# A step of the first stage emitted a slot later, with more buffers and another spacing of the weight work

## Chip, cores and metric

The kernel runs on 1 core of one Trainium2 chip. The metric is the device time of one execution in microseconds (us). Before the change it is 957.8 us, the median of 3 runs (956.14 to 958.7).

## What is computed

Linear attention with 128 random features, then two feed-forward layers. Cut to what matters here:

```
def phi(x):                                   # features of keys and of queries
    proj = einsum('bhsd,md->bhsm', x, omega)
    h = proj - sum(x*x)/2
    return exp(h - max(h, axis=-1)) / sqrt(m)
kv  = einsum('bhsm,bhsd->bhmd', phi(k), v)    # per batch and head: values by features
num = einsum('bhsm,bhmd->bhsd', phi(q), kv);  den = einsum('bhsm,bhm->bhs', phi(q), sum(phi(k)))
x = num / den                                 # (4, 8, 576, 64) -> 2304 tokens x 512
x = (silu(xn @ w_gate) * (xn @ w_val)) @ w_out        # xn: rms norm of x; d_ff 1536
y = (h * cos(h)) @ w_out2,  h = x @ w_in              # d_ff 2048
```

## The kernel before, in words

Tokens go in 18 tiles of 128. The first stage walks 24 slots: in each one tile begins, 18 tiles of keys (named k0 to k17) and the first 6 tiles of queries (q0 to q5, in the slots 6, 9, 12, 15, 20 and 23). `begin(s)` of a slot emits `project` (L426: 16 matmuls on TensorE into two banks of PSUM, one for each half of the heads) and `features` (L435 and L437: VectorE reduces the maximum of each head out of the bank, two reductions a tile, and ScalarE runs 8 exponentials a tile, for which it needs those maxima). A key tile's features then go into `kv_product` (L591 before the change, 32 matmuls: values by features), which before the change is emitted in the slot after the tile's own. A query tile passes 7 further steps in later slots (`query_step`): 1 transposes its features (L444) and copies them (L454 on VectorE, L452 on ScalarE), 2 multiplies them with the sums of a batch and divides (L466, L476 to L478), 3 squares (L485), 4 takes the root (L489, L490, GpSimd), 5 scales (`norm`, L494, VectorE, at the head of its slot), 6 and 7 turn the result and split it (L504, L516, L518).

Within a slot the order is: loads that are due, step 5, `begin`, the other steps of older tiles, `kv_product`, and last `wts.tick(n)`. The tick takes n steps of the preparation of the first twelve chunks of weights, each 128x512 and loaded as 64-bit numbers, which `front` and `split` turn into a high and a low part. The steps run in a fixed cycle of eight, one cycle a chunk: L190 (VectorE, reads the tile W, writes f); L214 of the chunk before (ScalarE); L193 (VectorE; nothing for two chunks in three); L217 of the chunk before (GpSimd); L195 (VectorE); `exponent` of the next chunk (ScalarE, L182 or L184, writes W); L204 (VectorE); L209 (GpSimd). The tile W has one buffer. So `exponent` is the sixth step of a cycle, and the L190 that reads its W is the first of the next, three steps on. What the ticks have not done by the end of the slots is drawn later, at a rate (`pace`), between the products of layer 1.

Each engine has one queue and works through it in the order in which the code emits. Banks: `project` and the turned tile share four banks in a ring ("wa" and "wb"), so a `project` waits until the bank was read by the exponentials of two slots earlier, and, in the slots after a turned tile, until L518 has read that one. Features have 5 buffers (3 of the pool "att", 2 of "values"), values 3 (`vt`). SyncE's queue issues the loads; a load of values waits for the `kv_product` that read the buffer.

After the slots the first products of layer 1 follow (L833, L872 to L874, L886), with the steps of the other 12 query tiles among them; then the rest of the two layers, where TensorE is busy nearly all the time.

Of the kernel before, what the change touches and what calls it, by code (L numbers as in the profile page):

```python
# [33 lines left out]
F32 = mybir.dt.float32  # L34
# [10 lines left out]
P = 128  # L45
NB = 384
# [10 lines left out]
def attention_then_ffn(ctx: ExitStack, tc: tile.TileContext, qT, kT, v, omT, wc1, rms_g, wc2, out, B, H, S, D):  # L57
    nc = tc.nc
    M = omT.shape[1]
    DM = H * D  # L60
    KD = DM // P
    HP = H // 2
# [21 lines left out]
    def parts(t):  # L84

        pr, i = divmod(t, TPP)
        if i == MIX:
            return [(2 * pr, 0, P // 2), (2 * pr + 1, P // 2, P // 2)]
        return [(2 * pr + (i > MIX), 0, P)]
# [312 lines left out]
    wts = Weights()  # L402
# [144 lines left out]
    with tc.manual_schedule():  # L547
        fp = ctx.enter_context(tc.tile_pool(name="fp", bufs=2, reuse_waits="tile"))
        early = ExitStack()
        ap = early.enter_context(tc.tile_pool(name="att", bufs=2, side="right", reuse_waits="tile"))  # L550
        depth = {"gain": 1, "raw": 3, "feat": 3, "mx": 6, "den": 4}
        with_keys = {"raw": 1, "feat": 2}
        turn_of = {"raw": 0, "feat": 0}
        keys = [True]

        def att_tile(what, shape, dt, name):
            own = depth.get(what, 2)
            if keys[0] and what in with_keys:
                n = turn_of[what] % (own + with_keys[what])
                turn_of[what] += 1  # L560
                if n >= own:
                    return vp.tile(shape, dt, tag=what, name=name, bufs=with_keys[what])
            return ap.tile(shape, dt, tag=what, name=name, bufs=own)

        kv = [ap.tile([P, KVW], F32, name=f"kv{b}", bufs=1) for b in range(B)]
        NV = 3
        values = ExitStack()
        vp = values.enter_context(tc.tile_pool(name="values", bufs=1, side="right", reuse_waits="tile"))
        vt = [vp.tile([P, H, D + 1], F32, name=f"v{i}", bufs=1) for i in range(NV)]
        att = Attention(att_tile, "q", kv)  # L570


        acc = {}

        def load_v(t):
            if t < NTILE:
                nc.sync.dma_start(vt[t % NV][:, :, 0:D], v[t])

        def kv_product(t, i):
# [3 lines left out]
            for r in range(2):  # L583
# [3 lines left out]
                for h in range(HP):  # L587
                    hh = 2 * h + r
                    for c in range(2):
                        half_c = slice(c * M // 2, (c + 1) * M // 2)  # L590
                        nc.tensor.matmul(  # L591
                            acc[b, r][half_c, h * P:h * P + D + 1], att.e["k", t, r][p0:p0 + n, h, half_c],
                            vt[t % NV][p0:p0 + n, hh, :],
                            start=begin and h == 0, stop=end, skip_group_check=True)
# [148 lines left out]
        SLOTS = len(tiles)  # L743
# [3 lines left out]
        begins, then = {}, {}  # L747
        for s, (nm, t) in tiles.items():
            if nm == "k":
                for i in range(len(parts(t))):  # L750
                    then.setdefault(s + 1 + i, []).append((1, kv_product, t, i))
                then.setdefault(s + 2 + i, []).append((0, load_v, t + NV))
            else:
                for i in range(1, 8):
                    at = s + i + (s >= SLOTS - 1 or i > 1)
                    then.setdefault(at, []).append((-i, query_step, t, i))
# [6 lines left out]
        def load_ahead(s):  # L763
            at = order.index(s) if s in tiles else -1
            if at >= 0 and at + AHEAD[0] < len(order) and at + AHEAD[0] not in asked:
                asked.add(at + AHEAD[0])
                att.load(*tiles[order[at + AHEAD[0]]])

        def older(s, *steps):
            for step in steps:  # L770
                for k, f, *args in then.get(s, []):
                    if k == step:
                        f(*args)

        def begin(s):
            if s in tiles:
                att.project(*tiles[s])
                for r in range(2):
                    att.features(*tiles[s], r)
# [21 lines left out]

        for s in range(SLOTS):
            load_ahead(s)
            if s in (0, 1):
                load_v(s + 1)
                wts.load(s + 1, nc.sync)
            if s == 3:
                att.load_gain()
            older(s, 0, -5)
            begin(s)  # L810
            older(s, -7, -6, -4, -3, -1, -2, 1)
            if s:
                wts.tick(5 if s < 6 else 1 if s < 14 else 4 if s + 1 < SLOTS else 0)


        att.tag = "w"
# [48 lines left out]
        def silu(blk, f, ps):  # L865
            a = row(F32, f"gv{blk}_{f}")
            nc.scalar.activation(a, ps, AF.Silu)
            return a
# [82 lines left out]
        for n, (g, blk, f, first, last) in enumerate(steps):  # L951
# [9 lines left out]
            s = SLOTS + 2 * n  # L961
# [3 lines left out]
            a = silu(blk, f, ps)  # L965
# [466 lines left out]
```

## Time and profile before

| | |
|---|---|
| median of 3 runs | 957.8 us (956.14 to 958.7) |
| the profiled execution | 955.29 us, its span 953.5 us, mean granted clock 0.996 |
| TensorE (PE) busy | 929.5 us, 97% of the span |
| VectorE (DVE), ScalarE (ACT), GpSimd (POOL) | 713.4, 537.1, 415.5 us |
| chain that ended last | PE 43% of the span, beginning only at 497 us |

The span begins with the first instruction and ends with the last; 1.8 us of the execution lie around it. A row of a timeline gives start, duration and how many instructions it merges, and in brackets the idle time of the engine before it and what ended that.

### The profile page before, as it was taken

What the parts mean: (1) busy time and instruction counts of PE and PEld (TensorE: products, weight loads), DVE (VectorE), ACT (ScalarE), POOL (GpSimd) and SP (SyncE); (2) the same over time, 40 slices, a digit from 0 to 9 for tenths busy, and PEclk for the clock granted to TensorE, in tenths of its full rate; (3) what the DMA queues carried; (4) which work ended last, traced back from release to release, by engine and by line L of the source; (5) the groups of instructions that cost most, each with busy time, mean ns of one, the idle gap of its engine ahead of it and who ended that gap; (6) DMA issues with size and microseconds to landing.
All of it is one profiled execution on the core that took longest, in us unless ns stands there. A gap on an engine that the chain in (4) does not pass through costs nothing. (4 is left out here: it accounts for less than half of the span.)

```text
span 953.5 us, 17373 instructions
## 1 busy us (share of the span) xinstructions
PE 929.5 (97%) x6337; PEld 866.7 (91%) x6337; DVE 713.4 (75%) x1159; ACT 537.1 (56%) x1155; POOL 415.5 (44%) x377
## 2 busy tenths in 40 slices
PE   8988999999999999999999999999999999999998
PEld 7777998989999999999999998889888988988997
DVE  5797777878854685585876658996799787786766
ACT  7898776756535443435363645664655565464443
POOL 2143387467836975376583763320343220240000
PEclk9999999989999999999999999999999999999999
DMA  9774378777796988766989693967622767307554
GB/s 290 201 192 164 134 264 292 264 257 271 231 346 226 400 288 294 268 200 202 386 297 383 231 374 130 355 211 251 210 93 101 251 205 285 124 21 282 191 227 160
DMA packets 112214, 227.71 MB, mean 239 GB/s; under 512 B 28160, under 2 KB 63616, under 8 KB 112128
## 3 DMA queue, kind: packets, MB, share of 16 engines
q1 hardware_dynamic: 110832, 222.34, 67.5%
q10 hardware_dynamic: 1296, 4.26, 1.4%
q8 instruction: 50, 0.82, 0.4%
q14 instruction: 36, 0.29, 0.1%
HBM read 156.04 MB, written 70.52 MB: 238 GB/s over the span
## 5 line engine op out<-in xcount | busy, mean ns | idle before, releaser
L1253 PE MATMUL o_ps<-w,o 128*128 128x512 f32 x864 | 226.0, 393 | 0.7 <-DVE o L1056 0.7
L209 POOL TENSOR_TENSOR f<-f,raw 128x512 f32<-128x512 f32 x68 | 94.4, 1388 | 229.2 <-DVE raw L204 199.2
L1253 PEld LDWEIGHTS o_ps<-w,o 128*128 128x128 f32 x864 | 159.7, 188 | 24.5 <-DVE o L1056 1.1
L217 POOL TENSOR_TENSOR w<-b,w 128x512 fp32r<-128x512 f32 x88 | 115.5, 1318 | 137.0 <-ACT w L214 113.7
L833 PE MATMUL gv_ps<-xhl,w 128*128 128x384 f32 x576 | 109.3, 338 | 1.3 <-DVE eT L454 1.1
L833 PEld LDWEIGHTS gv_ps<-xhl,w 128*128 128x128 f32 x576 | 101.6, 190 | 2.4 <-DVE eT L454 1.6
L1152 PE MATMUL y<-t,w 128*128 128x384 f32 x576 | 102.0, 334 | 0.3 <-POOL w L217 0.3
L1152 PEld LDWEIGHTS y<-t,w 128*128 128x128 f32 x576 | 100.0, 188 | 0.6 <-POOL w L217 0.6
L1053 ACT CAST o<-turns 128x384 fp32r<-128x384 f32 x96 | 47.4, 513 | 93.4 <-DVE turns L1234 93.4
L1045 PE MATMUL Xh<-T,w 128*128 128x384 f32 x432 | 87.4, 336 | 1.6 <-ACT h L1198 1.6
L1045 PEld LDWEIGHTS Xh<-T,w 128*128 128x128 f32 x432 | 76.8, 188 | 9.7 <-ACT h L1198 4.1
L1045 PE MATMUL X<-T,w 128*128 128x384 f32 x432 | 80.7, 334 | 0.0
L1045 PEld LDWEIGHTS X<-T,w 128*128 128x128 f32 x432 | 75.4, 188 | 0.0
L214 ACT CAST w<-b 128x512 fp32r<-128x512 f32 x88 | 50.5, 580 | 31.9 <-DVE b L274 24.8
L1056 DVE TENSOR_TENSOR o<-turns,o 128x384 fp32r<-128x384 f32 x96 | 60.0, 639 | 8.5 <-ACT o L1053 8.1
L886 PE MATMUL y_ps<-t,w 128*128 128x384 f32 x288 | 61.8, 350 | 0.3 <-ACT t L873 0.3
L1019 ACT ACTIVATE turns<-turns,half_pi 128x768 f32<-128x768 f32 (+1 forms) x50 | 45.7, 914 | 22.8 <-DVE turns L1223 22.7
L1045 PE MATMUL Yh<-B,w 128*128 128x384 f32 x288 | 58.0, 336 | 0.0
L1223 DVE SCALAR_TENSOR_TENSOR turns<-turns,r 128x768 f32<-128x768 int32 (+1 forms) x50 | 56.4, 1128 | 1.7
L1234 DVE TENSOR_TENSOR turns<-h,turns 128x768 f32<-128x768 f32 (+1 forms) x50 | 55.1, 1101 | 2.5 <-ACT turns L1019 2.5
L190 DVE TENSOR_SCALAR f<-W 128x512 int32<-128x512 int32 x68 | 44.0, 647 | 15.1 <-ACT W L182 6.5
L1045 PEld LDWEIGHTS Yh<-B,w 128*128 128x128 f32 x288 | 51.4, 188 | 4.2 <-ACT h L1198 0.4
(116 smaller groups left out, 1804.6 us busy)
## 6 DMA issues: line engine op xcount, KB each, us to landing
T<-T_dram SPq DMA_DIRECT2D x48, 768.0 KB, 7.1
raw<-wc SPq DMA_DIRECT2D x60, 512.0 KB, 5.1
B<-yh_dram SPq DMA_DIRECT2D x21, 768.0 KB, 5.5
kept<-f SPq DMA_DIRECT2D x56, 256.0 KB, 5.1
b<-kept SPq DMA_DIRECT2D x56, 256.0 KB, 4.8
B<-x_dram SPq DMA_DIRECT2D x15, 768.0 KB, 6.7
x_dram<-xhl SPq DMA_DIRECT2D x12, 768.0 KB, 5.7
s<-x_dram SPq DMA_DIRECT2D x24, 384.0 KB, 5.6
```

Source lines behind the costliest of these rows:

```text
L209: nc.gpsimd.tensor_tensor(f32(f), f32(f), rest, op=ALU.add)
L214: nc.scalar.copy(t[:, 0, to], src)
L217: nc.gpsimd.tensor_tensor(t[:, 1, to], src, f32(t[:, 0, to]), op=ALU.subtract)
L833: nc.tensor.matmul(o, w[i], x[j], start=n == 0, stop=n == len(terms) - 1)
L886: nc.tensor.matmul(yacc[blk][e], w[:, i, e * P:(e + 1) * P], t[:, j], start=first and i + j == 0, stop=last and j == 1)
L1045: nc.tensor.matmul(o, w[:, i, c + kk * P:c + (kk + 1) * P], x[:, j, kk], start=begin and n == 0, stop=n == 5, skip_group_check=True)
L1053: nc.scalar.copy(t[:, 0], a)
L1056: engine.tensor_tensor(t[:, 1], a, f32(t[:, 0]), op=ALU.subtract)
L1152: nc.tensor.matmul(acc[e], w[:, i, e * P:(e + 1) * P], t[:, j], start=f == fs[0] and i + j == 0, stop=f == fs[-1] and j == 1)
L1223: nc.vector.scalar_tensor_tensor(r, a, -TWO_PI_LO, b, op0=ALU.mult, op1=ALU.add)
L1234: at(mu, lambda: nc.vector.tensor_tensor(r, h, r, op=ALU.mult))
L1253: nc.tensor.matmul(oacc[blk][j], o[:, x, js], w[:, y], start=first and n == 0, stop=last and n == 2)
```

## The change

Five edits, all in the first stage. `kv_product` of a key tile is emitted two slots after the tile's own and not one (the last one in slot 23 at the latest), and the load into its buffer of values a slot later too. There are four buffers of values (`NV`), and the load of the fourth stands in slot 2. Features have 8 buffers: three more come out of the tag "t" of the pool "fp", which later holds tiles of layer 1. The gain of the norm is loaded in slot 8 and not in slot 3. `wts.tick` takes 4 steps in the slots 1 to 5 (5 before), 2 in the slots 6 to 13 (1 before) and 4 from slot 14 on, as before; by the end of the slots that is 72 steps, and 69 before.

```
-        with_keys = {"raw": 1, "feat": 2}
+        with_keys, vp_bufs = {"raw": 1, "feat": 5}, {"raw": 1, "feat": 2}
...
+                if n >= own + vp_bufs[what]:
+                    a = fp.tile([P, 2, NB], F32, tag="t", name=name, bufs=3).rearrange("p a c -> p (a c)")
+                    return a[:, 0:HP * M].rearrange("p (h m) -> p h m", m=M)
...
-        NV = 3
+        NV = 4
...
-                    then.setdefault(s + 1 + i, []).append((1, kv_product, t, i))
-                then.setdefault(s + 2 + i, []).append((0, load_v, t + NV))
+                    then.setdefault(min(s + 2 + i, SLOTS - 1), []).append((1, kv_product, t, i))
+                then.setdefault(s + 3 + i, []).append((0, load_v, t + NV))
...
+            if s == 2:
+                load_v(3)
...
-            if s == 3:
+            if s == 8:
                 att.load_gain()
...
-                wts.tick(5 if s < 6 else 1 if s < 14 else 4 if s + 1 < SLOTS else 0)
+                wts.tick(4 if s < 6 else 2 if s < 14 else 4 if s + 1 < SLOTS else 0)
```

What that does to the queues, at three places. In the rows, a name's first number is the tile or chunk (qmx3_0 belongs to q3, f5 and W5 to chunk 5). First VectorE between the reductions of k11 (slot 14) and those of q3 (slot 15), before:

```order
L195 TENSOR_SCALAR raw4_397<-f4_840 128x512
L494 SCALAR_TENSOR_TENSOR x1_804<-x1_804,ms1_879,gain_301 128x512
L435 TENSOR_REDUCE qmx3_0_964<-qp_ps3_0_953 128x4
L435 TENSOR_REDUCE qmx3_1_971<-qp_ps3_1_954 128x4
L476 TENSOR_SCALAR den2_0_987<-num_ps2_0_977 128x4
L477 RECIPROCAL den2_0_987<-den2_0_987 128x4
L478 TENSOR_TENSOR x2_986<-num_ps2_0_977,den2_0_987 128x4x64
L476 TENSOR_SCALAR den2_1_1000<-num_ps2_1_991 128x4
L477 RECIPROCAL den2_1_1000<-den2_1_1000 128x4
L478 TENSOR_TENSOR x2_986<-num_ps2_1_991,den2_1_1000 128x4x64
L204 SCALAR_TENSOR_TENSOR raw4_397<-raw4_397 128x512
L190 TENSOR_SCALAR f5_1022<-W5_947 128x512
```

and now:

```order
L204 SCALAR_TENSOR_TENSOR raw4_424<-raw4_424 128x512
L190 TENSOR_SCALAR f5_938<-W5_934 128x512
L494 SCALAR_TENSOR_TENSOR x1_790<-x1_790,ms1_867,gain_556 128x512
L435 TENSOR_REDUCE qmx3_0_954<-qp_ps3_0_943 128x4
L435 TENSOR_REDUCE qmx3_1_961<-qp_ps3_1_944 128x4
```

The L190 that reads W5 has moved from behind the reductions of q3 to ahead of them. On ScalarE the order there is the same in both kernels: the exponentials of k11, then L184 that writes W5, then the exponentials of q3.

Second TensorE at the end of slot 6 and in slot 7, before:

```order
L591 MATMUL kv_ps1_0_483<-v1_105,ke4_0_363 64x65 x8
L591 MATMUL kv_ps1_1_492<-v1_105,ke4_1_370 64x65 x8
L591 MATMUL kv_ps1_0_483<-v2_106,ke5_0_415 64x65 x8
L591 MATMUL kv_ps1_1_492<-v2_106,ke5_1_422 64x65 x8
L426 MATMUL kp_ps6_0_521<-om_73,kraw6_350 128x128
```

and now:

```order
L444 MATMUL eT_ps0_0_503<-ident_72,qe0_0_442 128x128 x4
L444 MATMUL eT_ps0_1_510<-ident_72,qe0_1_449 128x128 x4
L594 MATMUL kv_ps1_0_517<-v0_104,ke4_0_343 64x65 x8
L594 MATMUL kv_ps1_1_526<-v0_104,ke4_1_350 64x65 x8
L594 MATMUL kv_ps1_0_517<-v1_105,ke5_0_392 64x65 x8
L594 MATMUL kv_ps1_1_526<-v1_105,ke5_1_399 64x65 x8
L426 MATMUL kp_ps7_0_560<-om_73,kraw7_379 128x128
```

The same two products stood ahead of the projection of k6 and now stand behind the transposes of q0, ahead of the projection of k7.

Third ScalarE in layer 1, between the exponentials of q14 and the copy of its transposes (some 195 us into the span before), before:

```order
L437 ACTIVATE qe14_1_3030<-qp_ps14_1_3014,qmx14_1_3031 128x128 x4
L214 CAST w13_3054<-b13_2726 128x512
L867 ACT_TABLE_LOAD
L867 ACTIVATE gv3_0_3071<-gv_ps3_0_0_3058 128x384
L516 CAST xhl4_0_3078<-xT_ps12_3073 128x2x128
L516 CAST xhl4_1_3079<-xT_ps12_3073 128x2x128
L485 ACTIVATE sq13_3082,ms13_3083<-x13_2995 128x512
L184 ACTIVATE W22_3091<-raw22_2948 128x512
```

and now:

```order
L437 ACTIVATE qe14_1_3034<-qp_ps14_1_3018,qmx14_1_3035 128x128 x4
L184 ACTIVATE W22_3053<-raw22_2903 128x512
L214 CAST w13_3061<-b13_2732 128x512
L872 ACT_TABLE_LOAD
L872 ACTIVATE gv3_0_3078<-gv_ps3_0_0_3065 128x384
L516 CAST xhl4_0_3085<-xT_ps12_3080 128x2x128
L516 CAST xhl4_1_3086<-xT_ps12_3080 128x2x128
L485 ACTIVATE sq13_3089,ms13_3090<-x13_2999 128x512
```

The L184 that writes W22 has moved six instructions ahead, since the weight work is three steps further on; VectorE's L190 that reads it stands ahead of the two L518 that read the turned tile, in both kernels.

## Rows read from the trace of the kernel before

**Rows 1.** Busy times by stretch: us of each engine, clock, DMA share, GB/s.
```profile
10.90:82.70 71.80, 62.65 (x1163) 54.64 (x1159) 61.83 (x124) 64.04 (x217) 25.41 (x24) 1.00 0.82 234
```

**Rows 2.** Waits of ScalarE, 8 to 82.8 us: total, times, longest.
```profile
ACT ke L437 <- DVE kmx L435: 3.5, 6, 0.9
ACT w L214 <- POOL f L209: 2.8, 4, 1.0
ACT qe L437 <- DVE qmx L435: 0.9, 2, 0.7
ACT W L182 <- DVE f L190: 0.5, 1, 0.5
```

**Rows 3.** Timeline of ScalarE in the slots 1 to 6.
```profile
10.96 0.81 ACT L182 ACTIVATE W<-raw 128x512 f32<-128x512 f32 x1
...
13.32 2.18 ACT L437 ACTIVATE ke<-kp_ps,kmx 128x128 f32<-128x128 f32 x8 [0.37 <-DVE kmx L435]
...
23.65 0.85 ACT L182 ACTIVATE W<-raw 128x512 f32<-128x512 f32 x1
25.14 0.62 ACT L214 CAST w<-f 128x512 fp32r<-128x512 f32 x1 [0.64 <-POOL f L209]
...
26.03 2.18 ACT L437 ACTIVATE qe<-qp_ps,qmx 128x128 f32<-128x128 f32 x8 [0.27 <-DVE qmx L435]
```

**Rows 4.** Timeline of VectorE in the same slots.
```profile
11.79 0.43 DVE L190 TENSOR_SCALAR f<-W 128x512 int32<-128x512 int32 x1 [3.10 <-ACT W L182]
...
12.60 1.28 DVE L435 TENSOR_REDUCE kmx<-kp_ps 128x4 f32<-128x512 f32 x2
...
24.60 0.79 DVE L190 TENSOR_SCALAR f<-W 128x512 int32<-128x512 int32 x1 [0.87 <-ACT W L182]
```

**Rows 5.** Timeline of ScalarE behind k11 (slots 14 and 15).
```profile
51.73 0.74 ACT L184 ACTIVATE W<-raw 128x512 f32<-128x512 f32 x1
52.30 2.24 ACT L437 ACTIVATE qe<-qp_ps,qmx 128x128 f32<-128x128 f32 x8
```

**Rows 6.** Timeline of VectorE in the same slots: norm and L190.
```profile
49.80 0.75 DVE L494 SCALAR_TENSOR_TENSOR x<-x,ms,gain 128x512 f32<-128x512 f32 x1
...
53.95 0.42 DVE L190 TENSOR_SCALAR f<-W 128x512 int32<-128x512 int32 x1
```

**Rows 7.** Timeline of TensorE, slots 16 to 18, and the end of the slots.
```profile
54.35 1.04 PE L444 MATMUL eT_ps<-ident,qe 128*128 128x128 f32 x8
...
58.36 1.15 PE L591 MATMUL kv_ps<-v,ke 128*64 128x65 f32 x32
...
60.36 1.13 PE L426 MATMUL kp_ps<-om,kraw 64*128 64x128 f32 x14 [0.43 <-DVE xhl L518]
...
78.94 1.16 PE L426 MATMUL qp_ps<-om,qraw 64*128 64x128 f32 x14 [1.65 <-ACT ke L437]
...
82.04 4.43 PE L833 MATMUL gv_ps<-xhl,w 128*128 128x384 f32 x24
```

**Rows 8.** Timeline of VectorE in layer 1, the L190 near 199 us.
```profile
199.13 0.43 DVE L190 TENSOR_SCALAR f<-W 128x512 int32<-128x512 int32 x1 [3.60 <-ACT W L184]
```

**Rows 9.** Timeline of TensorE from 200 us.
```profile
200.32 0.46 PE L426 MATMUL qp_ps<-om,qraw 64*128 64x128 f32 x2 [1.76 <-issue]
201.20 2.07 PE L426 MATMUL qp_ps<-om,qraw 64*128 64x128 f32 x14 [0.43 <-DVE gv L872]
203.21 2.29 PE L886 MATMUL y_ps<-t,w 128*128 128x384 f32 x6
205.29 3.37 PE L833 MATMUL gv_ps<-xhl,w 128*128 128x384 f32 x12
...
209.67 1.34 PE L886 MATMUL y_ps<-t,w 128*128 128x384 f32 x6
210.84 2.24 PE L833 MATMUL gv_ps<-xhl,w 128*128 128x384 f32 x12
```

**Rows 10.** Busy times by stretch, as Rows 1, with the granted clock.
```profile
204.00:206.00 2.00, 2.00 (x8) 2.00 (x8) 1.97 (x3) 2.00 (x9) 1.92 (x3) 0.50 0.44 179
```

More of the change, by code (lines that the diff above doesn't have):

```diff
@@ L560, in att_tile @@
                 turn_of[what] += 1
+                if n >= own + vp_bufs[what]:
+                    a = fp.tile([P, 2, NB], F32, tag="t", name=name, bufs=3).rearrange("p a c -> p (a c)")
+                    return a[:, 0:HP * M].rearrange("p (h m) -> p h m", m=M)
                 if n >= own:
-                    return vp.tile(shape, dt, tag=what, name=name, bufs=with_keys[what])
+                    return vp.tile(shape, dt, tag=what, name=name, bufs=vp_bufs[what])
             return ap.tile(shape, dt, tag=what, name=name, bufs=own)
         kv = [ap.tile([P, KVW], F32, name=f"kv{b}", bufs=1) for b in range(B)]
-        NV = 3
+        NV = 4
         values = ExitStack()
```

## The prediction

> **What bounds the kernel now.** The page's busy shares come first: TensorE is busy for 97% of the span, so over most of it an edit that takes no matmul away can give nothing. The slices of the span then show where that is not so: in the first few, ScalarE is about as busy as TensorE, which it is nowhere later. The edits lie there. The busy times by stretch say it more sharply: from 10.9 to 82.7 us, ScalarE is busy 64.0 of 71.8 us, TensorE 62.7 and VectorE 61.8 [rows 1]. ScalarE is the fullest, but no engine is full: each waits for another in turn, and a slot ends when the loop of the three ends. So the third view is ScalarE's waits in that stretch. They sum to 7.7 us: 4.4 for the maxima of VectorE, 2.8 for GpSimd's sum of a chunk, 0.5 for VectorE's L190 [rows 2]. That is all that any edit of the order can give here, while ScalarE's work stays what it is. Last come the timelines of the three engines, which say which wait ends last in a slot.
>
> What TensorE's projection needs is a bank that ScalarE has read; what ScalarE's exponentials need is VectorE's reduction; and VectorE works in order. An instruction of VectorE that waits for ScalarE therefore holds up the reduction behind it, and with that ScalarE's own next exponentials. The trace has one such place in slot 5 and one in slot 1: L190 reads the tile W which ScalarE writes only after the exponentials of the slot. In slot 1 W starts at 10.96 [rows 3], L190 at 11.79 after 3.10 us of idling, the reduction behind it at 12.60 [rows 4], and the next exponentials at 13.32 [rows 3]. In slot 5 it is 23.65, 24.60 and 26.03 [rows 3, 4].
>
> **The change part by part.** *The spacing of the weight work.* One cycle of eight steps serves a chunk; `exponent`, which writes W, and the L190 that reads it are three steps apart. Counted through with the ticks of before (5 a slot, then 1, then 4), both fall into one slot only in the slots 1 and 5. With the new ticks (4, then 2, then 4) they do so in the slots 1, 2, 4, 14, 16, 18, 20 and 22. In each of these L190 now stands ahead of the next slot's reductions. Slots 14 and 15 show it: before, W5 starts at 51.73 and q3's exponentials follow it at 52.30, with no wait [rows 5], since L190 comes only at 53.95, behind those reductions [rows 6]. Now the exponentials of q3 must wait for W, L190, a norm and a reduction.
>
> The price of a pair: from the start of W to the start of L190 0.83 us [rows 3, 4], L190 0.43, the first reduction half of 1.28, so 0.64 [rows 4]: 1.90 in all, of which ScalarE works 0.57 on W (51.73 to 52.30) [rows 5]. It idles 1.33 us. The nearest rows give 0.91 in slot 5 (0.64 and 0.27, with another conversion in the gap) and in slot 1, from W's end to 13.32, 1.79 without the filling [rows 3]; I take 1.33 and keep 0.9 and 1.45 as ends. Six pairs lie ahead of the last keys: 8.0. Behind those of slots 14 and 20 a norm of 0.75 [rows 6] stands between L190 and the reduction: 1.5 more. In slot 1 the idle time was partly filled by the second W; that now comes behind the next exponentials, so 1.8 us are idle there. In all 11.3.
>
> *`kv_product` a slot later.* In a slot without queries this takes a matmul group of 1.1 us [rows 7] out of the way from one tile's exponentials to the projection two tiles on, and that is what the waits for maxima partly are. But behind a query tile the order within a slot is transposes first, `kv_product` last, and the transposes wait for that tile's exponentials. In slot 7 two products now stand behind them. From the end of q0's exponentials (26.03 plus 2.0) [rows 3] it takes half the transposes 0.5, two products 2.2, a projection 1.16 [rows 7] and half a reduction 0.64 [rows 4] to the exponentials of k7: 32.5. ScalarE has work until 31.1 (k6 2.0, a copy 0.5, W 0.57): it idles 1.4. When I walk the other slots in the same way, with these durations and the new order, waits of 0.2, 0.9 and 0.6 remain, at q2, k10 and k14, each behind a busy VectorE: 1.7.
>
> All 7.7 us of the waits before [rows 2] are replaced by these: 11.3 + 1.4 + 1.7 - 7.7 = 6.7 us, by which the exponentials of k17 come later. The walk in start times gives 5.3, as its durations of ScalarE come out a little short; the sum by waits doesn't depend on them. Behind k17 TensorE has one product more than before, as those of k16 and k17 now both stand in slot 23, ahead of the first matmuls of layer 1, which begin at 82.04 [rows 7]: 1.1. So layer 1 begins 7.8 us later.
>
> *Buffers and loads.* The eight buffers of features and the fourth of values only keep the later product from stopping the next tile: nothing by themselves. The three borrowed ones are read last in slot 23, ahead of the first tile of layer 1 that takes their place. The gain is loaded five slots later, still four slots ahead of the first norm. The loads of values wait for a product that has been emitted a slot later, and the next tile's load is queued behind them on SyncE; both have three slots of lead. The last values now queue behind the first big store and have two slots to land; if that is not enough, TensorE waits in slot 23, by 0 to 2 us (estimate, from slots of some 3.5 us). I take 0.
>
> *Layer 1.* The weight work is three steps further at the end of the slots, which shifts it against the products. Near 199 us, L190 holds VectorE for 3.60 us [rows 8], since W22 stands behind a table load and five others on ScalarE; TensorE then idles 1.76 and 0.43 us, and the groups after it run at 2.07, 2.29 and 3.37 us [rows 9] where the same groups take 1.16 [rows 7], 1.34 and 2.24 [rows 9]: 3.0 us more, at a granted clock of 0.50, the 1.2 GHz level [rows 10]. In the new order W22 stands ahead of those six. VectorE then waits only for the split of the turned tile, and by ScalarE's queue TensorE's idle time halves: 1.1 us less (0 to 2.2), and I take the drop of the clock to go too: 3.0 less. Elsewhere the shift turns one such order bad (q8) and one good (q11), by some 0.6 us each way.
>
> *The clock in the slots.* With L190 late, the turned tile's L518 is late: in slot 17 it stands behind the reductions of k13, and the projection of k14 waits for it. Before, that wait was 0.43 [rows 7]; in the walk it is 4.3 us of idle TensorE. Idle times of 1.76 and 0.43 were followed by the lower clock [rows 9, 10], though 1.65 alone was not [rows 7]. I take one drop, at half its price because TensorE is not what every slot waits for: 1.5 (0 to 9).
>
> **Sum.** 7.8 - 1.1 - 3.0 + 1.5 = 5.2 us. On the profiled execution (955.3, with 1.8 around its span) that is 960.5. It lies 2.5 below the median of the runs, on which the result is measured: 957.8 + 5.2 = 963.0.
>
> **Rivals.** *It evens out (same).* Pairs cost only the 0.91 of slot 5 and the clock does not drop in the slots: with p for a pair, the sum is 6p + 1.5 + 1.8 + 1.4 + 1.7 - 7.7 + 1.1 - 4.1, so 6p - 4.3; at 0.91 that is +1.2, 959.0. For it speaks that conversions can fill a gap; against it that most of the new gaps have none.
>
> *The pairs cost nothing (faster).* VectorE is 86% busy [rows 1]. If it reaches each L190 as late as at 53.95, 2.2 us after W began [rows 5, 6], W is done, p is 0, and the way freed of `kv_product` shows: -4.3, and with slot 8 hidden too -5.7, so 952 to 953.5. It decides from p below 0.23. Against it: in the new order little stands between the exponentials' reductions and L190, so VectorE must be early.
>
> *The clock falls several times (slower still).* Idle stretches of TensorE near 2 us also come in the walk in slots 4 and 22. Three drops at 3.0 instead of the half make 963.0 - 1.5 + 9.0 = 970.5. The Trainium skill ("TensorE: Matmul & The Clock Gate", Part 1, What's actually happening) says that a gate halves the array's clock by how busy it has been recently, half being the default that activity lifts; the rows near 200 us agree. By that rule alone the longer gaps of the slots would each bring the lower clock, which is this rival; the gap of 1.65 us without a drop [rows 7] speaks against it.
>
> **Chances.** Forecast 0.45 (its own range 960.7 to 968), evening out 0.25, faster 0.15, clock 0.15. Some 0.3%, 2.9 us, can be told from no change: slower 0.60, same 0.25, faster 0.15. The range takes the low end of the evened case with the second part of the faster one left out, 955, and the clock case's own time at the top, 970.
>
> **What would show it.** In the trace of the changed kernel, VectorE's L190 should wait for ScalarE's W six to eight times ahead of 90 us, near 1 us each or longer where it idles since the reductions; ScalarE's waits for maxima should be 10 us and more, where 4.4 stand now; k7 should begin its exponentials 1.5 to 2 us later; layer 1 should begin at 87 to 91 us; the wait of 3.60 near 199 should be gone and with it the low clock there. It is wrong if layer 1 begins ahead of 82 us, or if the late start is given back before the end.

## The result

The changed kernel takes 968.4 us, the kernel before 957.0 in the same comparison: a ratio of 1.0119, with a 95% interval of 1.0078 to 1.0159, so 11.4 us slower. The forecast was 963.0 us and slower, with 970 as the upper end of its range. The direction and the mechanism held; the size was about twice the forecast, just above the forecast's own range (960.7 to 968) and nearer to its rival with several drops of the clock (970.5). The profiled execution of the changed kernel has a span of 967.8 us, where that before had 953.5. Those 14.3 us are what the traces can explain; 2.9 us of them come from which executions were profiled (before 1.7 below its median, after 1.2 above).

**Where the time went.** The same matmul can be found in both traces, and the difference of its two start times says how much is lost up to there:

| first matmul of | before (us) | after (us) | later by |
|---|---|---|---|
| layer 1 (gate and value product) | 82.04 | 94.79 | 12.75 |
| layer 2 | 290.05 | 301.64 | 11.59 |
| the output product | 577.22 | 589.56 | 12.34 |
| end of the span | 953.5 | 967.8 | 14.3 |

Nearly all of it is lost in the slots, in the first tenth of the kernel. The busy times of the stretch of [rows 1] (us of TensorE, its weight loads, VectorE, ScalarE and GpSimd; then the granted clock, the DMA share and GB/s), in the changed kernel:

```profile
10.90:82.70 71.80, 62.14 (x1032) 55.09 (x1034) 53.84 (x109) 55.34 (x186) 22.74 (x23) 0.88 0.73 208
```

ScalarE was busy for 64.0 of these 71.8 us, and is so for 55.3 now; VectorE lost as much, 61.8 to 53.8. Both wait more for each other. The mean granted clock fell from 1.00 to 0.88. The waits of ScalarE from 8 to 90 us (total, times, longest), which answer to [rows 2]:

```profile
ACT ke L437 <- DVE kmx L435: 15.4, 11, 2.8
ACT qe L437 <- DVE qmx L435: 2.3, 2, 1.8
```

The waits for maxima are 17.7 us where they were 4.4 (one more, of 1.09 us ahead of q5, lies at 91.49 us, behind this window); those for GpSimd are gone from the list. What VectorE does meanwhile stands in the view of the line L190 from 0 to 100 us, "its engine sat idle before it (us, times) until":

```profile
L190 DVE TENSOR_SCALAR f<-W x10: 412/427/1377, 11.2 to 90.4; 128x512 int32<-128x512 int32 x10
...
  ACT W L182: 9.1, 5
  ACT W L184: 5.3, 3
```

Eight of ten L190 let VectorE idle until ScalarE has written W, 14.4 us in all; before, three of eleven did, 5.0 us in all. The slots 14 and 15 are the pair of which [rows 5, 6] show the state before. After the change, on ScalarE and then on VectorE:

```profile
53.73 0.73 ACT L184 ACTIVATE W<-raw 128x512 f32<-128x512 f32 x1
56.22 0.89 ACT L437 ACTIVATE qe<-qp_ps,qmx 128x128 f32<-128x128 f32 x3 [1.76 <-DVE qmx L435]
```
```profile
54.50 0.43 DVE L190 TENSOR_SCALAR f<-W 128x512 int32<-128x512 int32 x1 [1.83 <-ACT W L184]
54.84 0.75 DVE L494 SCALAR_TENSOR_TENSOR x<-x,ms,gain 128x512 f32<-128x512 f32 x1
55.51 1.28 DVE L435 TENSOR_REDUCE qmx<-qp_ps 128x4 f32<-128x512 f32 x2
```

L190 now stands ahead of the reduction of q3 and waits for W; the norm follows, then the reduction, and q3's exponentials wait 1.76 us, where before they followed W at once.

**The turned tile and the clock.** In slot 16 the same happens, and the copy L518 of the turned tile, behind L190 and the reductions on VectorE, comes late for TensorE. VectorE, then TensorE (rows of before: [rows 7]):

```profile
64.51 0.43 DVE L190 TENSOR_SCALAR f<-W 128x512 int32<-128x512 int32 x1 [2.79 <-ACT W L182]
64.85 1.28 DVE L435 TENSOR_REDUCE kmx<-kp_ps 128x4 f32<-128x512 f32 x2
66.05 0.75 DVE L518 TENSOR_TENSOR xhl<-xT_ps,xhl 128x256 fp32r<-128x256 f32 x2
```
```profile
66.94 2.04 PE L426 MATMUL kp_ps<-om,kraw 64*128 64x128 f32 x14 [4.26 <-DVE xhl L518]
68.91 2.00 PE L466 MATMUL num_ps<-kv,eT 128*64 128x65 f32 x32
70.70 1.95 PE L594 MATMUL kv_ps<-v,ke 128*64 128x65 f32 x32
```

The wait that was 0.43 us is 4.26 (the forecast's walk said 4.3), and the groups behind it take 2.0 us instead of 1.1. Their stretch, and one ahead of layer 1, with the granted clock as the third number from the end:

```profile
66.00:74.00 8.00, 7.06 (x95) 6.63 (x95) 5.54 (x15) 4.98 (x17) 2.67 (x2) 0.57 0.29 99
86.00:94.00 8.00, 6.18 (x90) 5.77 (x92) 6.54 (x15) 6.89 (x23) 2.56 (x2) 0.57 0.57 198
```

A mean of 0.57 means mostly the 1.2 GHz level. There are three shorter such stretches, near 15, 26 and 54 us; the trace of before has none ahead of 200 us.

The pair of slot 18 shows what that does. Its L190 finds W ready and doesn't wait; the reduction of k15 behind it waits for the projection, which stands behind the slow groups, and k15's exponentials with it (2.69 us). VectorE, then ScalarE:

```profile
72.31 0.42 DVE L190 TENSOR_SCALAR f<-W 128x512 int32<-128x512 int32 x1
74.05 1.29 DVE L435 TENSOR_REDUCE kmx<-kp_ps 128x4 f32<-128x512 f32 x2 [1.32 <-PE kp_ps L426]
```
```profile
74.77 0.89 ACT L437 ACTIVATE ke<-kp_ps,kmx 128x128 f32<-128x128 f32 x3 [2.69 <-DVE kmx L435]
```

**Behind the slots.** The wait of 3.60 us on VectorE near 199 us [rows 8] is gone, and with it the low clock of [rows 9, 10]: between the same two matmuls (196.82 and 208.15 us before, 209.54 and 216.72 now) the changed kernel is 4.15 us quicker, as forecast. But two new waits give it back. TensorE in layer 1, ScalarE at the same place; then VectorE and TensorE in the first part of the output product:

```profile
262.21 0.66 PE L504 MATMUL xT_ps<-ident,x 128*128 128x128 f32 x4 [2.12 <-ACT gv L872]
```
```profile
261.67 0.49 ACT L872 ACTIVATE gv<-gv_ps 128x384 f32<-128x384 f32 x1 [3.14 <-DMA y_dram<-y]
```
```profile
641.29 1.50 DVE L287 TENSOR_TENSOR b<-b,b 128x256 f32<-128x256 f32 x1 [1.73 <-POOL w L217]
642.71 0.55 DVE L1206 TENSOR_TENSOR h<-Yh,h 128x384 f32<-128x384 f32 x1
```
```profile
643.31 1.32 PE L1050 MATMUL Yh<-T,w 128*128 128x384 f32 x6 [0.90 <-DVE h L1206]
...
647.41 0.79 PE L1050 MATMUL Xh<-T,w 128*128 128x384 f32 x3 [1.39 <-ACT h L1203]
```

The first is a silu (gv) whose buffer a store of y still holds. ScalarE waited for it before, too, but 0.53 us. On SyncE a store of the weight work (L347) has moved from behind the stores of y to ahead of them; before, then after:

```profile
243.80 1.32 SPq L857 DMA_DIRECT2D y_dram<-y  x2
245.18 1.10 SPq L347 DMA_DIRECT2D kept<-f  x1
```
```profile
254.27 0.51 SPq L347 DMA_DIRECT2D kept<-f  x1
255.53 2.00 SPq L862 DMA_DIRECT2D y_dram<-y  x2
```

In the profiles of all fourteen kernels of this text this order goes with the wait: 1.85 to 3.45 us in the five with L347 ahead, 0.34 to 1.43 us in the nine with it behind; that it is the whole reason was not tried. The second is a step of the weight work, L287, which waits for GpSimd and now stands ahead of L1206, the instruction that TensorE waits for. By matching matmuls, 3.9 us are lost from 216.7 to 264.1 us, 2.3 of them at the first wait and the rest in smaller ones ahead of it, and 2.6 us at the second.

### The profile page after: what moved, and what is told of

Read it like the earlier page. It is cut to its first block, busy times and chain, and to the rows that moved or that the text cites. A ratio compares the mean times of both kernels' runs of the same rounds, so it can differ in the third digit from the quotient of the medians.

```text
span 967.8 us, 17335 instructions
## 1 busy us (share of the span) xinstructions
PE 935.7 (97%) x6337; PEld 872.2 (90%) x6337; DVE 715.9 (74%) x1160; ACT 536.2 (55%) x1155; POOL 413.0 (43%) x377
## 3 DMA queue, kind: packets, MB, share of 16 engines
q10 hardware_dynamic: 1296, 4.26, 1.3%
## 5 line engine op out<-in xcount | busy, mean ns | idle before, releaser
L1061 DVE TENSOR_TENSOR o<-turns,o 128x384 fp32r<-128x384 f32 x96 | 60.4, 644 | 10.9 <-ACT o L1058 10.4
L190 DVE TENSOR_SCALAR f<-W 128x512 int32<-128x512 int32 x68 | 46.8, 688 | 23.5 <-ACT W L182 12.0
L204 DVE SCALAR_TENSOR_TENSOR raw<-raw 128x512 f32<-128x512 uint32 x68 | 56.6, 832 | 0.5
```

Source lines behind the costliest of these rows:

```text
L204: nc.vector.scalar_tensor_tensor(rest, raw[:, :, 0].bitcast(U32), 2.0 ** -52, rest, op0=ALU.mult, op1=ALU.mult)
L1061: engine.tensor_tensor(t[:, 1], a, f32(t[:, 0]), op=ALU.subtract)
```

## Experiments

Two theories stood against each other. One: W and its L190 in one slot (a pair) make VectorE and ScalarE wait for each other, and the lower clock follows. The other: `kv_product` a slot later, with its buffers and queues, costs it. The first four runs take the two edits apart. In all of them W is what `exponent` writes.

**Old steps, later product.**

```
-  wts.tick(4 if s < 6 else 2 if s < 14 else 4 if s + 1 < SLOTS else 0)
+  wts.tick(5 if s < 6 else 1 if s < 14 else 4 if s + 1 < SLOTS else 0)
```

> The changed kernel with the steps of the weight work as before (5 a slot, then 1, then 4); kv_product, buffers and loads stay changed. Theory of the pairs (exponent, which writes W, and the L190 that reads it in one slot hold VectorE, and the late turned tiles then bring the lower clock): pairs are left in slots 1 and 5 alone, so most of the 12.75 us by which layer 1 began later goes. By the terms of the prediction 1.8 + 1.33 + 1.4 + 1.7 - 7.7 + 1.1 = -0.4: layer 1 begins near 82 us (80 to 85), no stretch at the 1.2 GHz level ahead of it, the wait near 199 us as in the kernel before, and the time is within 3 us of the kernel before. Rival, kv_product a slot later (with its buffers and its queue of loads) is the cost: layer 1 begins at 90 us or later and the time stays at +8 us or more.

It took 961.5 us, a ratio of 1.0064 (1.0041 to 1.0088). Layer 1 begins at 87.96 us, 5.9 later than before. So neither theory had it: half of the loss stays without the new steps, where the pairs' theory said none, and the low clock, which it said would not come, comes near 29, 53 and 75 us. TensorE, with the two products behind the transposes of q0 and those of slot 20 and 21:

```profile
25.71 2.04 PE L444 MATMUL eT_ps<-ident,qe 128*128 128x128 f32 x8 [1.41 <-ACT qe L437]
27.68 3.39 PE L594 MATMUL kv_ps<-v,ke 64*64 64x65 f32 x64
...
72.36 3.65 PE L594 MATMUL kv_ps<-v,ke 64*64 64x65 f32 x64
75.94 2.08 PE L426 MATMUL kp_ps<-om,kraw 64*128 64x128 f32 x16
```

Two products took 3.39 us at the first place and 3.65 at the second, where they take 2.23 at the 2.4 GHz level. ScalarE waited 3.42 us for k7 and 2.10 for k16 behind them.

**New steps alone.**

```
-  wts.tick(5 if s < 6 else 1 if s < 14 else 4 if s + 1 < SLOTS else 0)
+  wts.tick(4 if s < 6 else 2 if s < 14 else 4 if s + 1 < SLOTS else 0)
```

All else is the kernel before.

> The kernel before with the new steps of the weight work alone (4, then 2, then 4 a slot). Theory of the pairs: L190 waits for W in slots 1, 2, 4 and the even ones from 14 to 22, layer 1 begins 9 to 14 us later (91 to 96 us), with two to five stretches at the 1.2 GHz level ahead of it; the 4.1 us near 199 us are won; in all +6 to +12 us. Rival, kv_product later is the cost: layer 1 begins within 2 us of the kernel before, and with the gain near 199 us the time is 2 to 4 us below it.

964.4 us, a ratio of 1.0093 (1.0066 to 1.0119). Layer 1 begins at 89.70, a little earlier than the theory of pairs said. ScalarE's waits for maxima are 15.4 us (12.8 and 2.6), without that for q5, as above. The steps alone bring most of the loss. The two new waits of layer 1 and of the output product are there too (2.3 us of TensorE for gv, 2.6 us near 641), so they come from the steps, not from the product.

**No pair: with the later product, and with the earlier one.**

```
-  wts.tick(4 if s < 6 else 2 if s < 14 else 4 if s + 1 < SLOTS else 0)
+  wts.tick(1 if s == 1 else 4 if s < 6 else 2 if s < 14 else 4 if s + 1 < SLOTS else 0)
```

> The changed kernel with one step in slot 1, then 4 a slot to slot 5, 2 to slot 13, 4 after: W and its L190 then fall into one slot nowhere, and at the end of the slots 69 steps are done as in the kernel before. Theory of the pairs: ScalarE's waits for maxima fall from 17.7 us to below 6, layer 1 begins at 78 to 83 us, no low clock ahead of it; the wait near 199 us is there as before; time -4 to +1 us against the kernel before. Rival, spreading the weight work over the middle slots at 2 instead of 1 a slot is itself the cost, pairs or not: +5 us or more. Rival, kv_product later is the cost: +8 us.

> The kernel before with the same steps without a pair (1 in slot 1, then 4, 2, 4), kv_product where it was. Theory of the pairs: the waits of slots 1 and 5 go (near 1.8 + 0.9 us), the rest stays: layer 1 begins at 79 to 82 us, time -3 to +0.5 us against the kernel before. Against the run of the changed kernel with these steps it tells what kv_product later is worth by itself: by the prediction's terms +1.4 + 1.7 + 1.1 less some of the 4.4 us of waits for maxima, so within 2 us of each other.

With the later product 954.2 us, a ratio of 0.9989 (0.9975 to 1.0004), layer 1 at 81.94; with the earlier one 955.8 us, 1.0011 (0.9990 to 1.0032), layer 1 at 82.18. Both rivals fall: steps of two in the middle slots cost nothing, and with this spacing the later product costs nothing that the times show (with the old spacing it cost 6 us, so it isn't free everywhere). There are three steps fewer in slot 1, 69 in all, and every slot behind differs from the changed kernel by the phase alone. ScalarE's waits for maxima in the first of the two:

```profile
ACT ke L437 <- DVE kmx L435: 3.7, 6, 1.0
ACT w L214 <- POOL f L209: 3.3, 4, 2.0
```

3.7 us, where the changed kernel has 17.7.

**The same pairs, W ahead of the exponentials.** The steps, their number and their slots stay those of the changed kernel; in the slots with four, the first two move to the front of the slot.

```
+            if s and (s < 6 or 14 <= s < SLOTS - 1):
+                wts.tick(2)
             begin(s)
...
-                wts.tick(4 if s < 6 else 2 if s < 14 else 4 if s + 1 < SLOTS else 0)
+                wts.tick(2 if s + 1 < SLOTS else 0)
```

> The changed kernel with its steps of the weight work in the same slots and the same number (4, 2, 4; W and L190 in one slot in the slots 2, 4, 14, 16, 18, 20, 22, as there), but of each four the first two stand ahead of the slot's projection and reductions and the last two behind: W then stands ahead of the slot's exponentials on ScalarE, and L190 behind the slot's reductions on VectorE. Theory: a pair costs only because L190 waits for a W that stands behind the exponentials, so ScalarE's waits for maxima fall from 17.7 us to below 9, no or one stretch of low clock is left, layer 1 begins at 82 to 86 us instead of 94.8, and the time is 8 to 12 us below the changed kernel (-1 to +3 us against before); the order behind layer 1's start is that of the changed kernel. Rival: what costs is the amount of weight work in these slots (or kv_product): layer 1 begins at 91 us or later, +8 us or more against before.

959.1 us, a ratio of 1.0024 (1.0011 to 1.0038); layer 1 at 83.43 us. With the amount of work in each slot unchanged, 11.4 us of the 12.75 go, so what costs is that W stands behind the slot's exponentials and L190 ahead of the next reductions, with the waits and the low clock that came with it (here the clock is low near 10 and 52 us alone). Waits of ScalarE:

```profile
ACT ke L437 <- DVE kmx L435: 6.1, 8, 1.4
ACT qe L437 <- DVE qmx L435: 1.3, 3, 0.6
```

The 4.2 us near 199 are won here as well, and given back as in the changed kernel.

**One pair.**

```
+  wts.tick(1 if s == 1 else 4 if s < 6 else 2 if s < 14 else 7 if s == 16 else 1 if s == 17 else 4 if s + 1 < SLOTS else 0)
```

> The run without pairs (1, 4, 2, 4) with 7 steps in slot 16 and 1 in slot 17 instead of 4 and 4: one pair, W6 and L190 of chunk 6 both in slot 16; every other slot as there. By the price of the prediction, one pair makes k13 begin 1.33 us later than in the run without (0.9 to 1.45), measured against k12's start (4.41 us there); the later copies of the turned tile then leave TensorE idle for more than the 1.57 us there ahead of k14's projection, a stretch of low clock of 3.4 or 6.8 us behind it, and layer 1 begins 2 to 4 us later than at 81.9. If pairs cost nothing by themselves: k13 within 0.4 us and layer 1 within 1 us.

959.1 us, a ratio of 1.0036 (1.0022 to 1.0050). k13 begins 5.66 us behind k12, where the run without pairs has 4.41: the pair costs 1.25 us (forecast 1.33). VectorE, ScalarE and TensorE there:

```profile
58.12 0.43 DVE L190 TENSOR_SCALAR f<-W 128x512 int32<-128x512 int32 x1 [1.77 <-ACT W L182]
```
```profile
59.18 0.88 ACT L437 ACTIVATE ke<-kp_ps,kmx 128x128 f32<-128x128 f32 x3 [1.17 <-DVE kmx L435]
```
```profile
60.55 2.04 PE L426 MATMUL kp_ps<-om,kraw 64*128 64x128 f32 x14 [4.33 <-DVE xhl L518]
62.52 2.00 PE L466 MATMUL num_ps<-kv,eT 128*64 128x65 f32 x32
```

With the pair TensorE idles for 4.33 us here, and the clock is low from 58 to 66 us; without it, it idles 1.57 us, and the clock is low from 60 to 64. Layer 1 begins at 86.57, 4.6 us later than without, more than the 2 to 4 expected, and measured from k12 it is 6.4, as the profile without pairs was late at its start (see the last section). A second stretch of low clock, from 79 us, makes 2.9 of it; it stands behind 2.02 us of idling, and the run without pairs idles 2.00 there and keeps its clock, so it is open whether that stretch is the pair's. By the ratios (1.0036 and 0.9989) one pair costs some 4.5 us of time, so its own 1.25 us is the smaller part of its price. The seven steps in slot 16 instead of four were not tried without the pair.

**TensorE's idle time filled.** A helper issues matmuls of zeros into columns that nobody reads, ahead of the projections where TensorE idles; it shortens no wait.

```
+        def fill(n):
+            if acc:
+                ps = acc[max(acc)].rearrange("p (h c) -> p h c", c=P)[:, :, D + 1:P]
+                w = nothing.rearrange("p a c -> p (a c)")[:, 0:P]
+                for _ in range(n):
+                    nc.tensor.matmul(ps, w, nothing, start=False, stop=False, skip_group_check=True)
...
+            fill({15: 6, 18: 17, 23: 5}.get(s, 0))
             begin(s)
+            fill({22: 6}.get(s, 0))
```

> The changed kernel with TensorE's idle stretches of the slots filled: 6, 17, 6 and 5 matmuls of zeros (bf16, 252 columns, into columns of the values' bank that nobody reads) ahead of the projections of slots 15, 18 and 23 and in slot 22. They wait for nothing and shorten no wait. Theory A, the lower clock behind these idle stretches is a part of the loss: the stretches at the 1.2 GHz level from 52.7, 66.4 and 86.8 us (3.4 + 6.8 + 6.8 us) shrink or go, the groups behind them run at 1.0 to 1.2 us instead of 2.0, and layer 1 begins 3 to 6 us earlier than at 94.8, the time is 3 to 6 us less. Theory B, the waits of the pairs alone set the slots and the slow groups are hidden: layer 1 begins within 1.5 us of 94.8 and the time is the same as of the changed kernel (+11 us).

966.5 us, a ratio of 1.0115 (1.0095 to 1.0135), which can't be told from the changed kernel's 1.0119. In the profiled execution layer 1 begins at 91.56, 3.2 us earlier, and the mean clock of 10.9 to 82.7 us is 0.98 instead of 0.88. TensorE in the place of the 4.26 us:

```profile
61.28 2.06 PE L790 MATMUL kv_ps<-nothing 128*128 128x252 bf16 x17
63.27 0.48 PE L426 MATMUL kp_ps<-om,kraw 64*128 64x128 f32 x2
65.98 2.05 PE L426 MATMUL kp_ps<-om,kraw 64*128 64x128 f32 x14 [2.23 <-DVE xhl L518]
67.96 1.70 PE L466 MATMUL num_ps<-kv,eT 128*64 128x65 f32 x32
```

The gap was only half filled, and the low clock came all the same, for a shorter time. The trace speaks for the clock as a part of the loss of some 3 us, but the timing does not confirm it: theory A is not shown by this run alone (the last pair of runs below says more).

> The changed kernel with the old steps (the first run: +6.1 us, layer 1 at 88.0) and 5 matmuls of zeros in slot 7 ahead of the transposes of q0, 6 ahead of the projections of slots 15 and 18, 3 ahead of that of slot 20. Theory A, what kv_product later costs with the old steps is the lower clock, which meets the two products that stand ahead of k7 (28.4 to 31.8 us) and of k16 (72.7 to 79.5 us): k7 begins at 32.0 instead of 33.3, k16 two us earlier against k13, layer 1 at 83 to 85 us, the time +1 to +3 us. Theory B, the products cost this at either clock: layer 1 stays at 87 us or later.

The matmuls ahead of slots 15 and 18 ran, twelve in all; those of the slots 7 and 20 did not, since no bank of values is open there. 958.9 us, a ratio of 1.0030 (1.0018 to 1.0042), against 1.0064 without them; layer 1 at 85.38 instead of 87.96. The low clock near 29 us is still there and that near 53 and 75 is gone; k16 begins 6.78 us behind k15 instead of 8.70. So of the 6.1 us that the later product costs with the old steps, 2 to 3 go with the low clock that met the products ahead of k16 (8.70 and 6.78 us with it and without). The intervals of the two times just touch, and TensorE's idle time ahead of those products was not filled here: it is 0.86 us in both runs. That the matmuls of zeros kept the clock up there is therefore not shown. What is left stands at k7, in another place that wasn't filled (k7 begins 3.4 us late); whether the clock makes all of it was not tried.

> The run without pairs (1, 4, 2, 4 steps; 954.2 us) with 5, 4, 5 and 7 matmuls of zeros ahead of the projections of slots 15, 17, 18 and 23. Theory A: the low clock at 60.3 us goes, and with it up to 1.5 us (two groups at 2.00 and 1.63 instead of 1.15 and 1.10): layer 1 at 80 to 82 us, time 0 to 2 us less than without the matmuls. Theory B: no change within 1 us.

952.7 us, a ratio of 0.9967 (0.9948 to 0.9985): faster than the kernel before. Against the run without these matmuls (0.9989) the intervals overlap, and in the profiled executions layer 1 begins later with them (82.70 against 81.94), so their own gain isn't shown. The low clock at 60 us is gone, as theory A said, and another stretch, from 68 us, came.

**No pair, 71 steps.** Three steps in the slots 7, 9, 11 and 14, so that the slots end with 71 steps done instead of 69.

> The changed kernel with 1 step in slot 1, then 4, then 2 (3 in slots 7, 9, 11), 3 in slot 14, then 4: no slot holds W and its L190, and 71 steps are done at the end of the slots instead of 69 (72 in the changed kernel). Theory: pairs cost the slots, the number of steps done sets the order in the layers behind: layer 1 begins at 80 to 84 us; of the three places behind (near 199 us of before a wait of 3.6 on VectorE that the changed kernel doesn't have; 2.1 us of TensorE for gv at 262 us and 2.7 us near 641 us of the changed kernel that the kernel before doesn't have) it shows those of the changed kernel: -4 at the first, +2 and +2.7 at the others, so within 3 us of the kernel before. If these places don't hang on the steps done, it shows them as the run with 69 steps does.

957.9 us, a ratio of 1.0016 (1.0004 to 1.0029). Layer 1 begins at 86.35, later than expected, though k14 is where it is before: the norm of q3, which stands ahead of k16's reductions, starts only at 74.08, behind two steps of the weight work and a wait of 0.44 us for GpSimd, and takes 1.78 us; k16 waits 2.56 us:

```profile
74.08 1.78 DVE L494 SCALAR_TENSOR_TENSOR x<-x,ms,gain 128x512 f32<-128x512 f32 x1 [0.44 <-POOL ms L490]
```

A stretch of low clock near 83 us adds to it: from k17 to layer 1 it takes 6.85 us, 4.29 before. So pairs are not the only order that costs. Behind it, the stall near 199 is gone, and the wait for gv is there:

```profile
253.60 0.66 PE L504 MATMUL xT_ps<-ident,x 128*128 128x128 f32 x4 [2.23 <-ACT gv L872]
```

The 2.6 us of the output product are not (matmuls that lie 19.39 us apart before lie 19.78 apart here, 21.96 in the changed kernel). The first two places go with 71 and 72 steps, the third with 72 alone: what the steps shift at the end of the slots is carried to 640 us.

**Products ahead of the transposes.**

```
-            older(s, -7, -6, -4, -3, -1, -2, 1)
+            older(s, -7, -6, -4, -3, 1, -1, -2)
```

> The run without pairs (1, 4, 2, 4) with kv_product emitted ahead of a slot's transposes and sums instead of behind them. Theory: the two products that stand behind the transposes of q0 in slot 7, and those of slot 21, are what kv_product later costs at full clock (k6 to k7: 3.95 us there, 3.06 with kv_product at its old place); ahead of the transposes they fill TensorE's wait for the query's exponentials: k6 to k7 in 2.6 to 3.3 us, layer 1 at 80 to 82 us, time 0 to 2 us below the run without pairs (954.2). Rival: the quotients and the norm behind the transposes come later by as much, and layer 1 begins at 82 us or later, no gain.

> The same with the matmuls of zeros of the run that was fastest so far (5, 4, 5 and 7 ahead of the projections of slots 15, 17, 18, 23; 952.7 us). If both gains add: 950.5 to 952.5 us, 3 to 5 us below the kernel before. If the matmuls of zeros only stand in the way once the products fill the idle time: the same as the run before or up to 1.5 us more.

Without the matmuls of zeros 955.3 us, 0.9998 (0.9987 to 1.0010): no gain, and from k6 to k7 it takes 4.20 us, not 2.6 to 3.3. k7's reduction there stands behind other waits once the products are out of its way. Layer 1 begins at 83.67; the expectation fails, and the rival's signs came. With them 953.6 us, 0.9974 (0.9964 to 0.9984), layer 1 at 80.39, and no low clock in the slots (a mean of 1.00 from 10 to 84 us, and 0.93 without them). TensorE at the end of the slots without them, then the stretch with them:

```profile
76.66 2.07 PE L426 MATMUL qp_ps<-om,qraw 64*128 64x128 f32 x14 [2.03 <-ACT ke L437]
78.67 3.73 PE L594 MATMUL kv_ps<-v,ke 128*64 128x65 f32 x64
```
```profile
10.00:84.00 74.00, 66.88 (x1234) 59.30 (x1230) 63.32 (x130) 67.06 (x223) 27.24 (x26) 1.00 0.81 232
```

Here the matmuls of zeros show a gain of their own: the two intervals just miss each other, the time is 1.7 us less, and the stretches of low clock near 61 and 80 us that the run without them has are gone. It is neither of the two sizes expected. This and the earlier run without pairs and with such matmuls are the two versions that beat the kernel before, by about 0.3%; both keep the later product, and neither has a pair. They can't be told from each other.

## Why the prediction was right, and where its size was off

*The pairs.* Right in mechanism, and in price for most. The clean ones cost 1.09 us of ScalarE's time (k3, k5, k13), the first one with a norm 1.76, and 1.25 when a single one is made; the forecast took 1.33, within 0.9 to 1.45, and 2.08 with the norm. The second one with a norm, in slot 20, cost more: ScalarE waits 2.78 us for k16, as VectorE's L204 and L190 there took 1.69 and 1.38 us while GpSimd worked (last section), 0.68 and 0.43 elsewhere. The pair of slot 18 cost nothing by itself; late matmuls took its place. With W moved ahead of the exponentials, 11.4 us of the late start go.

*`kv_product` later.* Its 1.4 us at k7 came, where the clock allowed it: from k6 to k7 it takes 3.94 us in the changed kernel with its idle time filled, 2.47 before, 1.5 more, and ScalarE waits 1.28. In the changed kernel, with the low clock, it is 4.81, and the wait 2.15. That it would cost 6 us with the old steps was not foreseen.

*The sum in the slots.* New waits were put at 14.4 us (11.3 + 1.4 + 1.7) and are 17.7; k17 was to come 6.7 us later and comes 9.3 later; layer 1 was to begin 7.8 us later, or 9.3 with the clock term, and begins 12.75 later. **The first mis-sized term is the clock in the slots**: one drop at half price, 1.5. Five stretches came. Three of them meet what every slot waits for. Against the same kernel with its idle time filled, which ran most of the slots at the 2.4 GHz level, ScalarE waits 0.9 us more for k7 (2.15 and 1.28) and 1.4 more for k15 (2.69 and 1.29). From k17's start to layer 1 it takes 7.75 us instead of the 4.29 before, 3.5 more where the extra product was to cost 1.1; in the run without pairs, with the clock up, it takes 5.22, 0.9 more. Two of the new waits above the forecast are not the clock's: 0.7 more for k16 (2.78 where 2.08 were taken), and 1.05 for k12, which the walk did not have; both stand in the filled run as well. In that run layer 1 begins 9.5 us late, beside the forecast's 9.3 with one drop; it had two drops and these waits, so the agreement is in part luck.

*Layer 1 and behind.* **The second is the gain near 199 us.** Its 4.1 us were right (4.15) and are not kept: the prediction named one good and one bad order elsewhere at 0.6 each and looked no further than layer 1. The stretch up to the wait for gv near 262 and the wait for L287 near 641 give 3.9 and 2.6 back. In all, the time behind layer 1's start is 1.5 us more where the forecast had 4.1 less. 3.45 in the slots and 5.6 behind make the 9.1 us by which the profiled difference, 14.3, exceeds the 5.2 forecast.

*The signs.* L190 waits for W eight times, the waits for maxima are above 10 us, the wait near 199 us is gone, as named. Two came out larger than named: layer 1 begins at 94.79 us, not at 87 to 91, and k7 is 2.5 us later, not 1.5 to 2. That the time still lies within the range is owed to its upper end, which was set for the rival with several drops.

*The rivals.* That pairs cost nothing, or 0.91, is excluded by the waits. That the clock falls several times came true, on top of the forecast and not in its place. The rule of the Trainium skill that the prediction quotes ("TensorE: Matmul & The Clock Gate", Part 1, What's actually happening) fits most of these rows: the gaps of 4.26 and 4.33 us were followed by the 1.2 GHz level, and so was one of 1.63 us, ahead of 52.2 us in the changed kernel. But the 1.65 us of [rows 7] were not, nor were 2.00 us ahead of 77.90 in the run without pairs, while 2.02 us at the same place were in the run with one pair. The length of one gap did not tell it, and the prediction's one long gap was no ground for counting one drop, at half its price.

## What to carry to other kernels

When work is interleaved at so many steps a slot, look at which two steps fall into one slot: an instruction that reads what another engine writes at its slot's end holds up all that stands behind it. A price per wait is then only the start; ask which other engine goes idle through it, and what runs behind that at the lower clock. And a shift of interleaved work does not end with the stretch that is tuned: follow the order through the stages behind, to the last one.

## What the runs showed of the hardware

One program's profile differs between executions by the clock near its start: the run without pairs had the low clock at 9 us, and k6 began at 25.75; two others (with one pair, and with the products first), which are the same program up to there, had not, and k6 began at 23.97 and 24.06. Of that difference 0.5 to 0.6 us stand at k0 already (6.79, 6.19 and 6.26 us), ahead of the low clock. So nearly 2 us of a difference between two profiles of early slots can lie in the execution and not in the program.

Some of VectorE's instructions that read and write SBUF took 1 us longer beside GpSimd. L190 takes 0.43 us, and 1.38 when GpSimd's addition ran from 81.17 to 82.46; the reductions, which read PSUM, kept their 1.28 for two (at 59.24 us, while GpSimd worked from 58.99 to 60.46). VectorE, then GpSimd, of the changed kernel:

```profile
81.36 1.38 DVE L190 TENSOR_SCALAR f<-W 128x512 int32<-128x512 int32 x1 [0.85 <-ACT W L184]
```
```profile
81.17 1.29 POOL L209 TENSOR_TENSOR f<-f,raw 128x512 f32<-128x512 f32 x1
```

The Trainium skill ("SBUF — State Buffer", "SBUF: two separate sides") tells of a pair of ports that GpSimd shares with some of VectorE's instructions (those in a two-port mode or with two inputs from SBUF) as an exclusive lock, held for a whole instruction by whichever began first. L190 begins 0.19 us behind the addition and ends 0.28 us behind its end, which agrees; in which mode L190 ran, no trace here shows.
